# Expert stage of an attention, mixture-of-experts and feed-forward chain: the weight splits move behind the activation's halves, operand tiles are loaded a unit ahead, and the unit count is read sooner

## The chip, the cores and the metric

The kernel runs on one core of a Trainium2 chip. A core has five engines, each working through its own queue of instructions in order: PE (matrix products), DVE (element-wise work on vectors), ACT (activations and copies), POOL and SP. Here SP only issues transfers and reads registers. The metric is the device time of one execution in microseconds (us); the lower the better.

## The reference

Three steps follow each other: attention with pooled keys, a mixture of 8 experts that takes one expert per token, and a gated feed-forward layer.

```python
def _moe_ref(x, modality_id, w_gate, modality_bias, w1, w2):      # x: 4608 tokens x 512
    logits = x @ w_gate + modality_bias[modality_id]
    e_idx = np.argmax(logits, axis=1)
    ...                                                            # gate_w: softmax at e_idx
    for e in range(8):
        mask = e_idx == e
        h = np.maximum(x[mask] @ w1[e], 0.0)                       # w1[e]: 512 x 1024
        out[mask] = gate_w[mask, None] * (h @ w2[e])               # w2[e]: 1024 x 512

def _moe2_ref(x, w_in, w_out):                                     # w_in 512 x 2048, w_out 2048 x 512
    h = x @ w_in
    g = h * np.clip(h + 3.0, 0.0, 6.0) / 6.0
    return g @ w_out
```

The weights w_in and w_out arrive as 64-bit floats, so they have to be converted on the chip.

## The kernel before

The attention stage ends at about 197 us and the feed-forward stage starts at about 651 us. Between them lies the expert stage, in which the change is made. Tokens of one expert stand together in rows of a table, and `unit` works on 400 of them with one expert's weights. This input gives 12 units: one written out ahead of a loop, eight passes of the loop `For_i`, and three written out behind it. How many passes there are stands in `nun`, a number that DVE computes during the first unit; each engine loads it into a register ahead of the loop.

Full precision is kept by splitting each operand into a rounded part and a remainder: `split` has ACT write the rounded part (`wh`, `xhi`, `hi`) and DVE the remainder (`wl`, `xlo`, `lo`), and a product is three MATMULs. A unit has eight steps f = 0 to 7, over slices of 128 hidden columns. In step f:

- `w_dma(f+3)`: SP issues the loads of slice f+3 of the two weight matrices into one of two buffers `ws`; it waits until the split of slice f+1 has read that buffer.
- `w_split(f+2)`: two pairs of `wh` (ACT) and `wl` (DVE), one for w1 and one for w2, into one of four buffers.
- `h_mm(f)`: 12 MATMULs into `ph`, then `hi` on ACT (the activation's rounded half) and `lo` on DVE (its remainder).
- `y_mm(f-1)`: 12 MATMULs that add slice f-1 to the four outputs `y`. It needs hi and lo of f-1.

So PE does h(0), h(1), y(0), h(2), y(1), ..., h(7), y(6), y(7). At f = 7 the next unit's tokens are transposed in four chunks (`transp`), two ahead of y(6) and two behind it. Each writes one of two PSUM tiles `pt`, and `xhi`, `xlo` (and for the first chunk also the copy `tkr`) must have read a tile before the third and fourth chunk may write it. A unit ends with four copies `yo` (two on ACT, two on DVE). PE's last MATMUL of a unit is the last of y(7).

Work for the feed-forward stage is woven in. In the loop each pass converts one slice of w_in: `conv_load` loads it as two tiles `cs`, `conv` makes two lists of 13 small operations, and `unit` runs up to five of them per step. In the two units behind the loop `wo_load` and `wo_conv` do the same for six tiles of w_out (`ds`, nine operations each). The order within each engine is the order in which this code is written.

Of the kernel before, what the change touches and what calls it, by code (L numbers as in the profile page):

```python
# [781 lines left out]
def moe1(tc, g, xr_d, tok_d, y_d, s_d, w1, w2, w_in):  # L782
# [4 lines left out]
    def pool(n, b, st=es_l, **kw):  # L787
        return st.enter_context(tc.tile_pool(name=n, bufs=b, reuse_waits="tile", **kw))
# [21 lines left out]
        s.pst = pool("pst", 2, es_p, space=PSUM)  # L810

    def open3():
        s.cv = pool("cv", 1)
        s.st2 = pool("cst", 2)

    def ps():
        return s.pst.tile([P, 512], F32, name="pt", tag="pt")
# [17 lines left out]
    def transp(c, pt):  # L835
        for t in range(4):
            nc.tensor.transpose(pt[:, t * T4:(t + 1) * T4], s.xg[:, t, c * P:(c + 1) * P], g.idn[:T4, :T4])
        if c == 0:
            nc.tensor.transpose(pt[0:4, NW:NW + T4], s.xg[:, :, GC + 1], g.idn[:T4, :T4])
        split(nc, s.xhi[c], s.xlo[c], pt[:, 0:NW])  # L840
        if c == 0:
            nc.scalar.copy(s.tkr, pt[0:4, NW:NW + T4])
# [7 lines left out]
    def w_split(f, cs=range(2)):  # L850
        for c in cs:
            split(nc, s.wh[f % 4][:, c], s.wl[f % 4][:, c], s.ws[f % 2][:, c])
# [12 lines left out]
        return nc.sync.dma_start(y_d.rearrange("(d p) n -> p d n", p=P)[:, :, bass.ds(col, NW)], s.yo)  # L865

    def conv_load(c, h):
        t = s.st2.tile([P, 4, P, 2], I32, name="cs", tag="cs")
        for b, ks, n in ((t[:, 1:3], slice(h, 4, 2), 0), (t[:, 0:4:3], slice(h, 4, 2), F2)):
            nc.sync.dma_start(b.rearrange("p k f w -> p k (f w)"), w32[:, ks, bass.ds(2 * P * c + n, 2 * P)])  # L870
        return t

    def conv(t):

        sh = [P, 4, P]
        a, m, ex = (s.cv.tile(sh, I32, name=n, tag=n) for n in ("a", "m", "ex"))
        x = s.cv.tile([P, 8, P], F32, name="wx", tag="wx")
        o = s.cv.tile([P, 7, 2, P], F32R, name="wq", tag="wq", bufs=2)
        v = nc.vector
        tt = lambda d, p, q, op: lambda: v.tensor_tensor(x[:, d], x[:, p], x[:, q], op=op)  # L880
        return o, f64_parts(nc, g, t[:, :, :, 1], t[:, :, :, 0], a, m, ex) + [
            lambda: v.tensor_tensor(x[:, 0:4], a.bitcast(F32), m.bitcast(F32), op=ALU.add),
            tt(4, 0, 3, ALU.add),
            tt(6, 1, 0, ALU.subtract),
            tt(5, 4, 1, ALU.subtract),
            tt(7, 2, 5, ALU.subtract),
            lambda: nc.scalar.copy(o[:, :, 0], x[:, 1:8]),
            lambda: v.tensor_tensor(o[:, :, 1], x[:, 1:8], o[:, :, 0].bitcast(F32), op=ALU.subtract),
        ]
# [1 line left out]
    def conv_store(o, c, h):  # L891
        nc.sync.dma_start(s_d[bass.ds(c, 1), :, h].rearrange("o s p x -> p (o s) x"), o.bitcast(F32).rearrange("p s w f -> p s (w f)"))

    def unit(i, first=False, last=False, tail=None, quad=None, fs=()):
        e = s.e0 if first else reg(0, i, E - 1)
        yps = [s.psy.tile([P, NW], F32, name=f"y{d}", tag=f"y{d}") for d in range(4)]
        hh = {}
        cs = {}

        def h_mm(f):  # L900
            j = f % 4
            n = 0
            ph = s.psh.tile([P, NW], F32, name="ph", tag="ph")
            for k in range(4):
                for a, b in ((s.wh, s.xhi), (s.wh, s.xlo), (s.wl, s.xhi)):
                    nc.tensor.matmul(ph, a[j][:, 0, k * P:(k + 1) * P], b[k], start=(n == 0), stop=(n == 11))  # L906
                    n += 1
            hi = s.hp.tile([P, NW], F32R, name="hi", tag="hi")
            lo = s.hp.tile([P, NW], F32R, name="lo", tag="lo")
            nc.scalar.activation(hi, ph, AF.Relu)  # L910
            nc.vector.scalar_tensor_tensor(lo, ph, 0.0, hi.bitcast(F32), op0=ALU.max, op1=ALU.subtract)  # L911
            hh[f] = (hi, lo)

        def y_mm(f):
            j = f % 4
            hi, lo = hh.pop(f)
            for d in range(4):
                for n, (a, b) in enumerate(((s.wh, hi), (s.wl, hi), (s.wh, lo))):
                    nc.tensor.matmul(yps[d], a[j][:, 1, d * P:(d + 1) * P], b, start=(f == 0 and n == 0), stop=(f == 7 and n == 2))  # L919

        lx = LX if first else 1
        parts = {LX: (0, 1, 2, 3)} if first else {1: (0,), 2: (1,), 3: (2,), 4: (3,)}
        ops = []
        for f in range(8):
            if first and f == 0:
                w_dma(e, 2)
            if f == lx and not last:
                en = reg(0, i + 1, E - 1)
            if f < 5 or not last:
                w_dma(e if f < 5 else en, (f + 3) % 8)  # L930
            if f == 0 and not first:
                col = reg(5, i, NT)
                if quad is not None:
                    cc = nc.values_load(g.tab[0:1, 6, bass.ds(quad, 1)], engines=(ET.SP,), min_val=0, max_val=NQ - 1)
            if f < 6 or not last:
                w_split((f + 2) % 8)
            h_mm(f)
            if f in parts and not last:
                load_x(i + 1, parts[f])
            if f - 1 in parts and not last:  # L940
                gate_x(parts[f - 1])
            if f == 2:
                store_tok(NT if first else reg(5, i + 1, NT))
            if f == 3 and not first:
                store_y(col)
            if f == 7 and not last:
                for c in range(2):
                    transp(c, ps())
            if f > 0:
                y_mm(f - 1)  # L950
            if tail and next(tail, None):
                open3()
            if last:
                if f in (1, 2):
                    g.y_load(0, f - 1)
                if f == 3:
                    ops = g.y_ops(0)
                if f == 3:
                    nc.sync.dma_start(g.tk, tok_d[NW:NW + NT].rearrange("(c p) -> c p", p=P))
                if f == 7:  # L960
                    pt = ps()
                    nc.tensor.transpose(pt[:, 0:NT // P], g.tk, g.idn[0:NT // P, 0:NT // P])
                    nc.vector.tensor_copy(g.tki, pt[:, 0:NT // P])
                if f >= 1:
                    g.s_load()
                if f >= 3:
                    for _ in range(3):
                        if ops:
                            ops.pop(0)()
                if f >= 6:  # L970
                    g.wo_load(REST[f - 6])
            elif quad is not None:
                if f == 0:
                    cs[0], cs[1] = conv_load(cc, 0), conv_load(cc, 1)
                if f == 1:
                    co, ops = conv(cs.pop(0))
                if f == 4:
                    c1_, ops = conv(cs.pop(1))
                for _ in range(5):
                    if ops:  # L980
                        ops.pop(0)()
                if f == 4:
                    conv_store(co, cc, 0)
                if f == 7:
                    conv_store(c1_, cc, 1)
            elif fs:
                if f in (0, 1, 4):
                    g.wo_load(fs[min(f, 2)])
                if f in (1, 3, 5):
                    ops += g.wo_conv(fs[f // 2])  # L990
                for _ in range(5):
                    if ops:
                        ops.pop(0)()
        if not last:
            for c in range(2, 4):
                transp(c, ps())
        y_mm(7)
        for d in range(4):
            (nc.scalar.copy if d % 2 else nc.vector.tensor_copy)(s.yo[:, d], yps[d])

    def run(tail):
        open_ps()
        unit(0, first=True, tail=tail)
        n_l = nc.values_load(g.nun, min_val=NQ, max_val=NQ + 8)
        with tc.For_i(0, n_l, 1, iteration_sync="reg_based") as i:
            unit(i + 1, quad=i)
        es_l.close()
        g.open_d()
        unit(n_l + 1, fs=EARLY[0:3])
        unit(n_l + 2, fs=EARLY[3:6])  # L1010
        unit(n_l + 3, last=True)
        store_y(reg(5, n_l + 4, NT))
        es_p.close()
        es_r.close()
# [171 lines left out]
def chunk_kernel(ctx, tc, q, k, v, mid, w_gate, mbias, w1, w2, w_in, w_out, out):  # L1186
# [8 lines left out]
    with tc.manual_schedule(engines={ET.PE, ET.Activation, ET.DVE, ET.SP}):  # L1195
# [5 lines left out]
            g.sp, g.yp, p, g.cv = pool("ds"), pool("dy"), pool("dw"), pool("dcv")  # L1201
            g.wo = {f: p.tile([P, 2, DM], F32R, name=f"wo{f}") for f in EARLY}

        g.open_d = open_d
        g.tk = g.cp.tile([NT // P, P], F32, name="tk")
        g.tki = g.cp.tile([P, NT // P], I32, name="tki")
        g.raw, g.yc = {}, {}
# [41 lines left out]
        g.sts = {}  # L1249

        def wo_load(f):
            t = g.yp.tile([P, DM, 2], I32, name="ds", tag="ds", bufs=2)
            nc.sync.dma_start(t.rearrange("p f w -> p (f w)"), w_out.bitcast(I32)[f * P:(f + 1) * P])
            g.sts[f] = t

# [40 lines left out]
```

## Time and profile before

| what | us |
|---|---|
| median of 3 runs | 1419.81 (1418.35 to 1423.13) |
| profiled execution, its own time | 1420.61 |
| its span, from the first to the last instruction | 1418.9 |
| PE busy | 1371.0 (97%) |
| DVE busy | 940.7 (66%) |
| ACT busy | 624.1 (44%) |
| a loop pass, from a unit's last MATMUL to the next unit's last | 36.42 to 36.44 |

The profile is one execution. Its own time is 1.7 us longer than its span, and 0.8 us above the median of the runs. A busy PE is not a PE at its peak, because the matmuls overlap; so for the expert stage the time of whole units says more than PE's busy share.

### The profile page before, as it was taken

How to read it: one execution, taken by the hardware profiler on the slowest of the kernel's cores; microseconds unless marked ns; L12 is line 12 of the kernel's file. 1: busy time of each engine (PE TensorE's matmuls, PEld its weight loads, DVE VectorE, ACT ScalarE, POOL GpSimd, SP SyncE). 2: the span in 40 equal slices, each digit the busy share in tenths (PEclk: the TensorE clock that was granted, in tenths of full speed). 3: DMA queues.
4: the chain of work that ended last, by engine and by line, in shares of the span. 5: the costliest groups of instructions: out<-in, count | busy, mean ns of one | idle time of the engine just before them, and what ended most of it. 6: DMA issues, size and time to landing. Idle time of an engine off the chain costs nothing.

```text
span 1418.9 us, 24229 instructions
## 1 busy us (share of the span) xinstructions
PE 1371.0 (97%) x7685; PEld 1263.2 (89%) x7685; DVE 940.7 (66%) x1922; ACT 624.1 (44%) x1262; POOL 156.5 (11%) x190
## 2 busy tenths in 40 slices
PE   7898999999999999999999999999999999999997
PEld 5787889899999999898888888888889888888886
DVE  6988884888888886777787445645654564455443
ACT  3666663555555554444444333423432342244222
POOL 3232341111111111100000100100010010001001
PEclk8999999999999999999999999999999999999999
DMA  9996265777778776665654544553454355445431
GB/s 247 305 299 190 91 198 161 237 242 242 240 243 248 241 242 199 198 210 179 202 162 119 183 137 123 157 165 114 122 181 141 113 150 176 119 116 166 115 116 67
DMA packets 229238, 253.87 MB, mean 179 GB/s; under 512 B 19225, under 2 KB 191293, under 8 KB 229149
## 3 DMA queue, kind: packets, MB, share of 16 engines
q1 hardware_dynamic: 223388, 232.64, 54.7%
q0 software_dynamic: 5760, 20.10, 3.9%
q8 instruction: 50, 0.82, 0.3%
q14 instruction: 40, 0.32, 0.1%
HBM read 206.21 MB, written 46.47 MB: 178 GB/s over the span
## 4 chain that ended last, share of the span: by engine, by line
issue 56%; POOL 2%; DVE 2%; DMA 1%; PE 1%; ACT 0%; SPq 0%; POOLq 0%; DVEq 0%; ACTq 0%
POOL out_dram L1049 2%; DMA ds<-in_moe_w_out_dram 1%; DVE wl L755 1%; DMA ws<-in_moe_w_dram 0%; PE ph L906 0%; DVE lo L911 0%; PE y L919 0%; DVE da L766 0%; DVE dex L777 0%; DVE dm L764 0%; DVE dm L765 0%; DVE dm L768 0%; SPq L820 0%; ACT dex L763 0%; POOLq L1291 0%
## 5 line engine op out<-in xcount | busy, mean ns | idle before, releaser
L1070 PE MATMUL hps<-yc,sq 128*128 128x384 f32 x2004 | 405.1, 337 | 3.3 <-ACT s L1111 1.6
L1070 PEld LDWEIGHTS hps<-yc,sq 128*128 128x128 f32 x2004 | 358.3, 188 | 37.3 <-ACT s L1111 5.5
L1060 PE MATMUL ops<-wo,gh 128*128 128x512 f32 x1152 | 358.5, 392 | 0.0
L1060 PEld LDWEIGHTS ops<-wo,gh 128*128 128x128 f32 x1152 | 211.4, 188 | 23.1
L1060 PE MATMUL ops<-wo,gl 128*128 128x512 f32 x576 | 228.7, 397 | 0.0
L1082 ACT ACTIVATE r<-c,three 128x384 f32<-128x384 f32 x144 | 88.8, 617 | 208.4 <-DVE c L1092 208.0
L755 DVE TENSOR_TENSOR wl<-ws,wh 128x512 fp32r<-128x512 f32 x192 | 132.8, 728 | 35.5 <-ACT wh L754 32.1
L1086 ACT CAST gh<-r 128x384 fp32r<-128x384 f32 x192 | 98.7, 514 | 129.4 <-DVE r L1083 128.0
L754 ACT CAST wh<-ws 128x512 fp32r<-128x512 f32 x192 | 114.5, 619 | 72.2 <-DMA ws<-in_moe_w_dram 54.4
L919 PE MATMUL y<-lo,wh 128*128 128x400 f32 x384 | 133.6, 348 | 1.8 <-DVE lo L911 1.7
L919 PE MATMUL y<-hi,wh 128*128 128x400 f32 x384 | 134.6, 350 | 0.6 <-ACT hi L910 0.5
L906 PE MATMUL ph<-xhi,wh 128*128 128x400 f32 x384 | 132.3, 344 | 2.0 <-PEq L1291 1.2
L906 PE MATMUL ph<-xlo,wh 128*128 128x400 f32 x384 | 132.8, 346 | 0.0
L906 PE MATMUL ph<-xhi,wl 128*128 128x400 f32 x384 | 132.6, 345 | 0.0
L919 PE MATMUL y<-hi,wl 128*128 128x400 f32 x384 | 132.0, 344 | 0.0
L1060 PEld LDWEIGHTS ops<-wo,gl 128*128 128x128 f32 x576 | 107.9, 187 | 23.1
L1087 DVE TENSOR_TENSOR gl<-r,gh 128x384 fp32r<-128x384 f32 x192 | 106.5, 554 | 27.6 <-ACT gh L1086 23.2
L1049 POOL DMA_INDIRECT out_dram<-osb,tki x36 | 35.3, 982 | 777.3 <-ACT osb L1047 745.4
L1083 DVE SCALAR_TENSOR_TENSOR r<-r,c 128x384 f32<-128x384 f32 x144 | 80.4, 558 | 55.1 <-ACT r L1082 53.2
L829 POOL TENSOR_TENSOR cxg<-cxg 100x512 f32<-100x512 f32 x48 | 56.7, 1184 | 348.4 <-PE ph L906 182.6
L1083 DVE SCALAR_TENSOR_TENSOR r<-r,hps 128x384 f32<-128x384 f32 x48 | 26.6, 554 | 97.7 <-ACT r L1082 97.6
L1082 ACT ACTIVATE r<-hps,three 128x384 f32<-128x384 f32 x48 | 27.9, 581 | 131.6 <-PE hps L1070 131.5
(214 smaller groups left out, 1903.6 us busy)
## 6 DMA issues: line engine op xcount, KB each, us to landing
sq<-sd SPq DMA_DIRECT2D x336, 256.0 KB
ws<-in_moe_w_dram SPq DMA_DIRECT2D x192, 256.0 KB, 3.9
sd<-wq SPq DMA_DIRECT2D x16, 896.0 KB
cxg<-xr SPq DMA_DIRECT2D x44, 225.8 KB
yd<-yo SPq DMA_DIRECT2D x12, 800.0 KB
yr<-yd SPq DMA_DIRECT2D x12, 768.0 KB
kv<-in_k_dram SPq DMA_DIRECT2D x16, 512.0 KB
kv<-in_v_dram SPq DMA_DIRECT2D x16, 512.0 KB
```

What stands on the lines that cost most here:

```text
L754: nc.scalar.copy(hi, src)
L755: nc.vector.tensor_tensor(lo, src, hi.bitcast(F32), op=ALU.subtract)
L829: nc.gpsimd.tensor_tensor(s.xg[:, t, 0:DM].rearrange("p (h x) -> p h x", x=D), v, s.xg[:, t, GC:GC + 1].unsqueeze(2).to_broadcast([T4, H, ...
L906: nc.tensor.matmul(ph, a[j][:, 0, k * P:(k + 1) * P], b[k], start=(n == 0), stop=(n == 11))
L919: nc.tensor.matmul(yps[d], a[j][:, 1, d * P:(d + 1) * P], b, start=(f == 0 and n == 0), stop=(f == 7 and n == 2))
L1049: i_ = nc.gpsimd.indirect_dma_start(out=out, out_offset=bass.IndirectOffsetOnAxis(ap=tki[:, c:c + 1], axis=0), in_=o, in_offset=None).ins
L1060: nc.tensor.matmul(pso[t_], gt[a][:, t * P:(t + 1) * P], wo[f][:, b], start=(q == 0 and fh == th and n == 0), stop=(q == NQ - 1 and fh != ...
L1070: nc.tensor.matmul(ps, w[:, kk, a * P:(a + 1) * P], y[:, b, kk], start=(start and n == 0), stop=(n == 5), skip_group_check=True)
L1082: a_.activation(r, c, AF.Relu, bias=g.three)
L1083: v.scalar_tensor_tensor(r, r, 6.0, c, op0=ALU.min, op1=ALU.mult)
L1086: a_.copy(gh, r)
L1087: late.append(lambda: v.tensor_tensor(gl, r, gh.bitcast(F32), op=ALU.subtract))
```

## The change

Three things change in `unit`. The weight split of a step is written behind `h_mm`, so `hi` and `lo` stand ahead of it on ACT and DVE; at f = 7 it stands behind the first two transposed chunks. The tiles `cs` for a pass are loaded during the unit before it: the first two, together with two tiles of w_out, in the first unit at f = 3, and each following one as soon as its buffer has been read; the conversions then start at f = 0, and run four operations per step in the w_out units instead of five. And `nun` is loaded into the registers at f = 6 of the first unit. The two `ds` buffers get a pool of their own, opened early.

```diff
     def open3():
+        g.open_w()
         s.cv = pool("cv", 1)
-        s.st2 = pool("cst", 2)
+        p = pool("cst", 1)
+        s.cs = [p.tile([P, 4, P, 2], I32, name=f"cs{h}") for h in range(2)]
...
     def conv_load(c, h):
-        t = s.st2.tile([P, 4, P, 2], I32, name="cs", tag="cs")
+        t = s.cs[h]
...
-                    cc = nc.values_load(g.tab[0:1, 6, bass.ds(quad, 1)], engines=(ET.SP,), min_val=0, max_val=NQ - 1)
-            if f < 6 or not last:
-                w_split((f + 2) % 8)
+                    cc, cn = (nc.values_load(g.tab[0:1, 6, bass.ds(quad + d, 1)], engines=(ET.SP,), min_val=0, max_val=NQ - 1) for d in range(2))
             h_mm(f)
+            if f < 7:
+                if f < 6 or not last:
+                    w_split((f + 2) % 8)
...
             if f == 7 and not last:
                 for c in range(2):
                     transp(c, ps())
+                w_split(1)
             if f > 0:
                 y_mm(f - 1)
             if tail and next(tail, None):
                 open3()
+                for h in range(2):
+                    conv_load(0, h)
+                for w in EARLY[0:2]:
+                    g.wo_load(w)
+            if first and f == 6:
+                s.n_l = nc.values_load(g.nun, min_val=NQ, max_val=NQ + 8)
...
             elif quad is not None:
-                if f == 0:
-                    cs[0], cs[1] = conv_load(cc, 0), conv_load(cc, 1)
-                if f == 1:
-                    co, ops = conv(cs.pop(0))
-                if f == 4:
-                    c1_, ops = conv(cs.pop(1))
+                if f in (0, 3):
+                    co, ops = conv(s.cs[f // 3])
                 for _ in range(5):
                     if ops:
                         ops.pop(0)()
-                if f == 4:
-                    conv_store(co, cc, 0)
-                if f == 7:
-                    conv_store(c1_, cc, 1)
-            elif fs:
-                if f in (0, 1, 4):
-                    g.wo_load(fs[min(f, 2)])
-                if f in (1, 3, 5):
-                    ops += g.wo_conv(fs[f // 2])
-                for _ in range(5):
+                if f in (3, 6):
+                    conv_store(cq, cc, f // 3 - 1)
+                    conv_load(cn, f // 3 - 1)
+                if f in (2, 5):
+                    cq = co
+            elif fs is not None:
+                if f in (0, 2, 4):
+                    ops += g.wo_conv(EARLY[3 * fs + f // 2])
+                for _ in range(4):
                     if ops:
                         ops.pop(0)()
+                n = 3 * fs + f // 2 + 1
+                if f in (2, 4, 6) and n < len(EARLY):
+                    g.wo_load(EARLY[n])
...
     def run(tail):
         open_ps()
         unit(0, first=True, tail=tail)
-        n_l = nc.values_load(g.nun, min_val=NQ, max_val=NQ + 8)
+        n_l = s.n_l
```

On DVE, at the end of the first unit behind the loop (the ninth after the first), the program of before has these rows; `ds`, `da`, `dm`, `dex` and `wo` belong to the conversion of w_out:

```order
L911 SCALAR_TENSOR_TENSOR lo<-ph,hi 128x400
L768 SCALAR_TENSOR_TENSOR dm<-ds,dex 128x512
L777 TENSOR_TENSOR dex<-da,wo_3809 128x512
L778 TENSOR_TENSOR wo_3809<-dex,dm 128x512
L755 TENSOR_TENSOR wl_2597<-ws_2092,wh_2593 128x512 x2
L911 SCALAR_TENSOR_TENSOR lo<-ph,hi 128x400
L755 TENSOR_TENSOR xlo_2087<-pt,xhi_2083 128x400
L755 TENSOR_TENSOR xlo_2088<-pt,xhi_2084 128x400
```

The changed program has these at the same place:

```order
L910 SCALAR_TENSOR_TENSOR lo<-ph,hi 128x400
L755 TENSOR_TENSOR wl_2596<-ws_2091,wh_2592 128x512 x2
L777 TENSOR_TENSOR dex<-da,wo_3830 128x512
L778 TENSOR_TENSOR wo_3830<-dex,dm 128x512
L910 SCALAR_TENSOR_TENSOR lo<-ph,hi 128x400
L755 TENSOR_TENSOR xlo_2087<-pt,xhi_2083 128x400
L755 TENSOR_TENSOR xlo_2088<-pt,xhi_2084 128x400
L755 TENSOR_TENSOR wl_2597<-ws_2092,wh_2593 128x512 x2
```

Between the last two `lo` there were three conversion operations and two `wl`; now two `wl` and two operations, and the step's own `wl` pair stands behind the first two `xlo`.

On ACT, at the head of a loop pass, the program of before has these rows (`ex` is the first operation of a w_in conversion):

```order
L754 CAST wh_2594<-ws_2091 128x512
L754 ISA
L754 CAST wh_2594<-ws_2091 128x512
L910 ISA
L910 ACTIVATE hi<-ph 128x400
L754 CAST wh_2595<-ws_2092 128x512
L754 REGISTER_ALU
L754 CAST wh_2595<-ws_2092 128x512
L910 ISA
L910 ACTIVATE hi<-ph 128x400
L763 REGISTER_ALU
L763 ACTIVATE ex<-cs 128x512
```

and the changed program these:

```order
L909 ACTIVATE hi<-ph 128x400
L754 CAST wh_2594<-ws_2091 128x512 x2
L763 ACTIVATE ex<-cs_3077 128x512
L909 ISA
L909 ACTIVATE hi<-ph 128x400
L754 CAST wh_2595<-ws_2092 128x512 x2
L909 ISA
L909 ACTIVATE hi<-ph 128x400
```

Each `hi` now comes ahead of the `wh` pair of its step, and `ex` one step sooner.

On SP, in the first unit, these rows of before lie between the loads of slices 6 and 7:

```order
L848 DMA ws_2091<-in_moe_w_dram 128x512
L820 TENSOR_LOAD tab
L820 ISA x2
L846 ISA
L846 DMA ws_2092<-in_moe_w_dram 128x4x128
```

and these in the changed program:

```order
L850 DMA ws_2091<-in_moe_w_dram 128x512
L872 DMA cs_3077<-in_moe_w_in_dram 128x2x256 x2
L872 DMA cs_3078<-in_moe_w_in_dram 128x2x256 x2
L1261 DMA ds<-in_moe_w_out_dram 128x1024 x2
L822 TENSOR_LOAD tab
L822 ISA x2
L848 ISA
L848 DMA ws_2092<-in_moe_w_dram 128x4x128
```

Six transfers, 2 MB in all, are issued there that were issued later before.

## Rows read from the trace of the kernel before

**Rows 1.** The page, part 1: busy us (share) x instructions of each engine.

```profile
PE 1371.0 (97%) x7685; PEld 1263.2 (89%) x7685; DVE 940.7 (66%) x1922; ACT 624.1 (44%) x1262; POOL 156.5 (11%) x190
```

**Rows 2.** Units 0, 1, 2, 9, 10: length; busy PE, PEld, DVE, ACT, POOL; clock; DMA.

```profile
197.34:237.85 40.51, 38.74 (x228) 36.13 (x224) 27.40 (x97) 18.41 (x42) 10.55 (x10) 1.00 0.56 171
237.85:279.44 41.59, 37.93 (x211) 36.01 (x211) 30.17 (x53) 18.87 (x35) 4.93 (x4) 1.00 0.74 225
279.44:315.86 36.42, 36.42 (x211) 36.32 (x210) 29.69 (x53) 19.12 (x35) 4.43 (x4) 1.00 0.78 243
...
534.46:577.87 43.41, 39.03 (x210) 37.01 (x210) 31.13 (x52) 19.52 (x37) 4.91 (x4) 0.97 0.66 199
577.87:616.04 38.17, 37.41 (x210) 36.82 (x210) 31.67 (x52) 19.36 (x37) 5.25 (x4) 0.98 0.60 184
```

**Rows 3.** Timeline, PE, unit 0: start us, us, instruction [idle before <-releaser].

```profile
203.46 0.45 PE L919 MATMUL y<-lo,wh 128*128 128x400 f32 x1 [0.59 <-DVE lo L911]
...
231.99 0.45 PE L919 MATMUL y<-lo,wh 128*128 128x400 f32 x1 [0.18 <-DVE lo L911]
```

**Rows 4.** Timeline, all engines, from unit 0 into the loop.

```profile
238.23 0.49 ACT L999 COPY yo<-y 128x400 f32<-128x400 f32 x1 [0.60 <-PE y L919]
...
238.85 0.45 PE L906 MATMUL ph<-xhi,wh 128*128 128x400 f32 x1 [0.65 <-ACTq L1005]
```

**Rows 5.** Timeline, ACT, unit 1 (the loop's first pass).

```profile
248.13 0.66 ACT L763 ACTIVATE ex<-cs 128x512 f32<-128x512 f32 x1 [3.96 <-DMA cs<-in_moe_w_in_dram]
```

**Rows 6.** Timeline, PE, unit 1: the product behind it, and the transposes.

```profile
252.71 0.45 PE L919 MATMUL y<-hi,wh 128*128 128x400 f32 x1 [0.51 <-ACT hi L910]
...
275.97 0.56 PE L837 MATMUL pt<-idn,cxg 100*128 100x100 f32 x4 [1.24 <-ACT tkr L842]
```

**Rows 7.** Timeline, all engines, end of unit 9.

```profile
567.39 0.35 PE L906 MATMUL ph<-xhi,wl 128*128 128x400 f32 x1
...
572.06 0.57 DVE L911 SCALAR_TENSOR_TENSOR lo<-ph,hi 128x400 fp32r<-128x400 f32 x1
...
573.43 0.57 PE L837 MATMUL pt<-idn,cxg 100*128 100x100 f32 x4 [2.46 <-ACT tkr L842]
```

**Rows 8.** Windows, the stretch after that wait.

```profile
575.00:580.00 5.00, 5.00 (x20) 5.00 (x20) 2.27 (x5) 2.52 (x5) 0.00 (x0) 0.66 0.27 91
```

**Rows 9.** Timeline, PE, out of the loop into unit 9.

```profile
536.02 0.42 PE L906 MATMUL ph<-xhi,wh 128*128 128x400 f32 x1 [1.21 <-PEq L1291]
```

**Rows 10.** Timeline, PE, the transposes at the end of unit 10.

```profile
613.61 0.56 PE L837 MATMUL pt<-idn,cxg 100*128 100x100 f32 x4 [0.43 <-DVE xlo L755]
```

**Rows 11.** Timeline, DVE, steps 0 and 1 of a loop pass (unit 6).

```profile
428.48 0.57 DVE L911 SCALAR_TENSOR_TENSOR lo<-ph,hi 128x400 fp32r<-128x400 f32 x1 [0.28 <-ACT hi L910]
428.97 1.28 DVE L755 TENSOR_TENSOR wl<-ws,wh 128x512 fp32r<-128x512 f32 x2
```

**Rows 12.** Timeline, PE, same pass: first MATMUL of h(2).

```profile
431.92 0.34 PE L906 MATMUL ph<-xhi,wh 128*128 128x400 f32 x1
```

**Rows 13.** Timeline, SP, unit 0: loads of slice 7 and of the next tokens.

```profile
217.45 0.38 SPq L846 DMA_DIRECT2D ws<-in_moe_w_dram  x1
...
219.27 5.60 SPq L824 DMA_DIRECT2D cxg<-xr  x4
```

**Rows 14.** Timeline, DVE, unit 0: the last operation on the unit table.

```profile
214.32 0.15 DVE L744 TENSOR_TENSOR urr<-urr,udf 32x4 f32<-32x4 f32 x1
```

**Rows 15.** Windows, unit 0: the transfers.

```profile
216.00:218.00 2.00, 2.00 (x13) 2.00 (x12) 1.91 (x6) 0.51 (x1) 0.00 (x0) 1.00 0.00 0
218.00:226.00 8.00, 8.00 (x46) 8.00 (x45) 2.23 (x4) 1.64 (x3) 2.13 (x2) 1.00 0.55 154
```

**Rows 16.** Tile cs, 230 to 300 us: time of its 256 KB loads.

```profile
DMA to landing us min/median/max: 2.9/4.7/5.9
```

**Rows 17.** Timeline, ACT and PE, unit 0: split and product of slice 7.

```profile
221.74 0.62 ACT L754 CAST wh<-ws 128x512 fp32r<-128x512 f32 x1 [3.99 <-DMA ws<-in_moe_w_dram]
...
227.93 0.35 PE L906 MATMUL ph<-xhi,wh 128*128 128x400 f32 x1
```

More of the change, by code (lines that the diff above doesn't have):

```diff
@@ L867, in conv_load @@
     def conv_load(c, h):
-        t = s.st2.tile([P, 4, P, 2], I32, name="cs", tag="cs")
+        t = s.cs[h]
         for b, ks, n in ((t[:, 1:3], slice(h, 4, 2), 0), (t[:, 0:4:3], slice(h, 4, 2), F2)):
             nc.sync.dma_start(b.rearrange("p k f w -> p k (f w)"), w32[:, ks, bass.ds(2 * P * c + n, 2 * P)])
-        return t
     def conv(t):
@@ L892, in conv_store, with unit @@
         nc.sync.dma_start(s_d[bass.ds(c, 1), :, h].rearrange("o s p x -> p (o s) x"), o.bitcast(F32).rearrange("p s w f -> p s (w f)"))
-    def unit(i, first=False, last=False, tail=None, quad=None, fs=()):
+    def unit(i, first=False, last=False, tail=None, quad=None, fs=None):
         e = s.e0 if first else reg(0, i, E - 1)
@@ L897, in unit @@
         hh = {}
-        cs = {}
         def h_mm(f):
@@ L1008, in run @@
         g.open_d()
-        unit(n_l + 1, fs=EARLY[0:3])
-        unit(n_l + 2, fs=EARLY[3:6])
+        unit(n_l + 1, fs=0)
+        unit(n_l + 2, fs=1)
         unit(n_l + 3, last=True)
@@ L1202, in open_d, with open_w @@
             g.wo = {f: p.tile([P, 2, DM], F32R, name=f"wo{f}") for f in EARLY}
-        g.open_d = open_d
+        def open_w():
+            g.dst = ctx.enter_context(tc.tile_pool(name="dst", bufs=2, reuse_waits="tile"))
+        g.open_d, g.open_w = open_d, open_w
         g.tk = g.cp.tile([NT // P, P], F32, name="tk")
@@ L1251, in wo_load @@
         def wo_load(f):
-            t = g.yp.tile([P, DM, 2], I32, name="ds", tag="ds", bufs=2)
+            t = g.dst.tile([P, DM, 2], I32, name="ds", tag="ds")
             nc.sync.dma_start(t.rearrange("p f w -> p (f w)"), w_out.bitcast(I32)[f * P:(f + 1) * P])
```

## The prediction

> **What bounds the kernel now.** I read the page first: PE is busy for 97% of the span, every other engine for less [rows 1]. So nothing can be won that doesn't shorten PE's waits, and the question is where those are. I therefore cut the expert stage into windows at each unit's last MATMUL [rows 2]. Unit 2, a loop pass, takes 36.42 us with PE busy for all of it, and the other passes behind the first take 36.42 to 36.44. That is what a unit costs when nothing makes PE wait. Against 36.43, unit 1 has 5.16 us too much, unit 9 has 6.98 and unit 10 has 1.74; unit 0, which carries other work as well, shows 1.77 us of idle PE. Units 2 to 8 have nothing to give back.
>
> Next I read PE's own timeline for the releaser of each wait. 211 MATMULs start in 36.42 us, so 0.17 us apart, while one lasts 0.34; a wait printed as x therefore costs about x + 0.16.
>
> - Unit 0: twice a second product waits for lo, 0.59 and 0.18 us [rows 3].
> - Into the loop: 0.65 us until ACT has signalled; its last copy yo starts at 238.23 and PE goes on at 238.85 [rows 4]. Between the two, ACT's queue holds the load of nun.
> - Unit 1: ACT waits 3.96 us for the first cs tile [rows 5]; behind that stand the next wh pair and the hi for which PE then waits. At the end the third transposed chunk waits 1.24 us for tkr [rows 6].
> - Unit 9: the product of step 7 has its last MATMUL at 567.39, but DVE comes to its lo only at 572.06, since conversions and two wl pairs stand ahead of it. xlo, tkr and PE's third chunk follow from there, and PE waits 2.46 us [rows 7]. After that wait PE's granted clock is 0.66 over 5 us, a mix of its two levels, full and half [rows 8]: 0.34 x 5 = 1.7 us of MATMUL time lost, part of it in unit 10's head.
> - Out of the loop into unit 9: 1.21 us for PE's sequencer [rows 9], which the change leaves.
> - Unit 10: the same transposes wait 0.43 us [rows 10], and as much again for the chunk before.
>
> **The change part by part.** *Splits behind hi and lo.* No instruction is added. A lo no longer stands behind a wl pair (1.28 us, [rows 11]), a hi no longer behind a wh pair that waits for a load. In unit 0 I count both late lo: 0.59 + 0.18 + 2 x 0.16 = 1.1, and 0.1 for the hi beside the second: 1.2 us. Bounds: 0, if DVE's backlog there comes from other work, and 2.7, all 1.77 us of idle PE with 0.16 for each of some six waits. The transposes of unit 0 I leave as they are.
>
> The price is that each split starts later, behind lo, and what is late next is the product that needs it. In a pass lo(0) starts at 428.48 and the next DVE operation at 428.97; a wl pair of 1.28 from there ends at 430.25 [rows 11], and h(2), which needs it, starts at 431.92 [rows 12]: 1.7 us to spare. Step 0 is the tightest, for from step 1 on a further product of 12 MATMULs (12 x 0.18 = 2.2 us) lies between. The load behind a split also starts later; two steps (four products, 8.7 us) lie between a buffer's splits, and the loads of such a size took at most 5.9 us [rows 16]. So I cost this at nothing for units 2 to 8.
>
> *Tiles a unit ahead.* In unit 1 the wait of 3.96 us on ACT goes, and with it the late hi and lo; the pass should then run as the others do. Of 5.16 us the loop's entry is 0.82 (0.65 + 0.16), so 4.35 us here. The lower bound is 2.9, if the wait at the transposes (1.24 + 0.16) comes back. In unit 9 the conversions start a step or two earlier and none is left at f = 7 but what the rows of the order show; the lo of step 7 stands right behind two of them. Of 6.98 us, 1.37 stay at the loop's exit (1.21 + 0.16), and I leave 0.3 for small waits: 5.3 us. Unit 10: all 1.7. Lower bounds: 1.3 and 0.5, if the long wait (2.46 + 0.16) and the clock's 1.7 stay in unit 9 and the transposes still wait in unit 10.
>
> The transfers themselves are the same ones earlier, plus one pass's 1 MB that nobody reads; the loop's transfers use 0.78 of the engines' time [rows 2]. Each pass reads one more register on SP. Four reads with their issues took 5.60 us [rows 13], so at most 1.4 us each. It is hidden while the load of slice 3 isn't needed before step 3; uncovered it would be 8 x 1.4 = 11 us.
>
> *nun sooner.* ACT's signal can follow its last copy's start instead of a load behind it. I take 0.5 of the 0.82 us (bounds 0 and 0.82). The load itself now stands ahead of hi(7) in unit 0, where ACT is busy for 18.41 of 40.51 us [rows 2].
>
> **Sum:** 1.2 + 4.35 + 0.5 + 5.3 + 1.7 = 13.05 us; with all upper bounds 15.2. The profiled execution took 1420.6, so 1407.5. It stands 0.8 above the median of the runs; I keep that as an allowance for waits a new order leaves.
>
> **The rivals.**
>
> *The 2 MB in unit 0 delay slice 7 (1410 to 1411.5).* Six loads now stand on SP ahead of it. The second cs tile lies where the unit table's scratch lay, so its loads wait for the table's last operation at 214.32 [rows 14]. Four issues remain then, of 0.38 us and a little between them, and the register read; slice 7 goes out at about 218.5 instead of 217.45 [rows 13]. The transfers were idle from 216 to 218 and half idle until 226 [rows 15]. At 243 / 0.78 = 311 GB/s 2 MB take 6.7 us, at 243 they take 8.6 [rows 2]. From 215.5 that ends at 222.2 or 224.1; slice 7's first half follows 1 us later, and its split takes 1.3: 224.5 to 226.5. Its product starts at 227.93 [rows 17], or 0.75 sooner with the first gain. So I expect no wait. A load was slower by 3 us when others stood around it (2.9 against 5.9, [rows 16]); so much again gives a wait of 2.3, and if the clock falls as in unit 9, 4.0. The Trainium skill's page "DMA: Bandwidth & Descriptors", section "Queues, rings and completion order", says that one DMA engine takes the descriptors of a ring in order. By that rule slice 7 can't overtake the 2 MB, which speaks for this rival; the spread of the cs loads agrees, and by it alone the time lies between my sum and 1411.5.
>
> *The transposes still wait (1414).* The wh pair now stands between the xhi of the second and third chunk. If the chain lo, xlo, tkr stays as late in units 1, 9 and 10 because DVE's work is no smaller (31 us of 43 and 38, [rows 2]), 1.4 + 4.3 + 1.1 = 6.8 us of the gain are lost. Against it: after lo(7) only xlo is left, and the conversions are over.
>
> *A loop pass pays (slower, 1421 or more).* If the later splits make h(2), or another product, wait in each of eight passes, 1.63 us per pass eat the sum. It decides from the point where a wl pair ends 3.3 us later than worked out above (1.7 to spare, and 1.63). SP's extra read could do it. Against it: DVE is busy for 29.7 of 36.4 us in a pass, so 6.7 us are spare; waiting for lo(0) at its head costs about 2.
>
> *The stalls only move (no change, 1417 to 1420).* DVE's total is the same, and each unit's end could collect what its middle gave.
>
> **How the numbers follow.** Forecast 0.60, slice 7 0.15, transposes 0.10, no change 0.08, slower pass 0.07. A measurement tells from no change what exceeds about 0.3%, 4.3 us. The first three are faster by more: 0.85. The range reaches from all upper bounds (1405) past the slice 7 rival to the transposes' (1414.5); outside are the last two and a little of each tail.
>
> **What would show it.** In the new profile: units 1, 9 and 10 within 0.5 us of 36.9, 38.1 and 36.5 (splits and tiles right); no half clock in unit 9; the entry to the loop at 0.5 us start to start; unit 0 at 39.3. Wrong: any of units 2 to 8 above 36.6, or PE waiting in unit 0 for wl of slice 7.

## The result and the profile after

The changed kernel takes 1426.65 us (median of 7 runs, 1423.92 to 1427.93); the kernel before, timed beside it, 1419.81. The ratio is 1.0058 (95% interval 1.0046 to 1.0071), so it is slower, by 0.6% (6.8 us between the medians), where 12 us less were forecast. The profiled execution has a span of 1424.9 us against 1418.9.

The page of the changed kernel, part 1, answers to [rows 1]:

```profile
PE 1373.1 (96%) x7685; PEld 1261.8 (89%) x7685; DVE 939.2 (66%) x1922; ACT 614.0 (43%) x1262; POOL 153.6 (11%) x190
```

The busy sums tell nothing of 6 us. The windows do, cut at the same place of each unit as in [rows 2]: units 0 and 1, then the passes 2 to 8, and, from the same view asked for other stretches, units 9 and 10.

```profile
196.90:237.47 40.57, 38.46 (x228) 36.49 (x224) 27.82 (x96) 17.81 (x42) 10.99 (x10) 1.00 0.72 223
237.47:275.29 37.82, 37.13 (x210) 36.22 (x210) 29.19 (x53) 18.00 (x35) 4.20 (x4) 1.00 0.76 225
...
546.38:585.83 39.45, 36.91 (x211) 36.31 (x211) 31.73 (x52) 19.11 (x37) 4.95 (x4) 1.00 0.68 205
585.83:622.38 36.55, 36.55 (x210) 36.38 (x210) 31.12 (x52) 18.66 (x37) 4.82 (x4) 1.00 0.59 178
```

```profile
275.29:314.05 38.76, 37.37 (x211) 36.29 (x211) 29.88 (x53) 17.98 (x35) 4.79 (x4) 1.00 0.75 227
314.05:351.64 37.59, 36.87 (x211) 36.26 (x210) 29.49 (x53) 17.99 (x35) 4.35 (x4) 1.00 0.79 234
...
467.25:507.05 39.80, 37.90 (x210) 36.13 (x210) 29.57 (x53) 17.99 (x35) 4.38 (x4) 1.00 0.73 223
...
sum 271.09, PE 261.30 PEld 253.57 DVE 207.88 ACT 125.94 POOL 30.58; mean PE 37.33 PEld 36.22 DVE 29.70 ACT 17.99 POOL 4.37
```

Units 1, 9 and 10 are shorter by 3.8, 4.0 and 1.6 us, as meant. But the seven passes that had nothing to give back take 271.1 us together instead of 255.0: 2.3 us each, 16.1 in all. No engine works more in them, the clock is 1.00 and the share of the transfers is 0.73 to 0.79, against 0.78 in unit 2 of before. So it is waiting, and the next step is to see what for. ACT in unit 7, from hi of step 5 on:

```profile
489.44 0.51 ACT L909 ACTIVATE hi<-ph 128x400 fp32r<-128x400 f32 x1 [2.75 <-PE ph L905]
495.49 1.29 ACT L754 CAST wh<-ws 128x512 fp32r<-128x512 f32 x2 [5.54 <-DMA ws<-in_moe_w_dram]
498.59 0.94 ACT L887 CAST wq<-wx 128x896 fp32r<-128x896 f32 x1 [1.81 <-DVE wx L880]
499.44 0.50 ACT L909 ACTIVATE hi<-ph 128x400 fp32r<-128x400 f32 x1
```

ACT waits 5.54 us for the load of slice 7. The same wait, 3.7 to 4.8 us, stands at step 5 of each other pass. Behind it in ACT's order are a conversion's wq, which needs DVE's wx, and then hi(6); on DVE the wl pair, wx, wq and lo(6) queue up in the same way. PE pays at the end of the unit, at five places in a row: h(7) waits for the wh of slice 7, y(6) for hi(6) and for lo(6), and the two late transposes for tkr and xlo.

```profile
496.16 0.45 PE L905 MATMUL ph<-xhi,wh 128*128 128x400 f32 x1 [0.22 <-ACT wh L754]
499.99 0.45 PE L918 MATMUL y<-hi,wh 128*128 128x400 f32 x1 [0.24 <-ACT hi L909]
501.20 0.45 PE L918 MATMUL y<-lo,wh 128*128 128x400 f32 x1 [0.58 <-DVE lo L910]
503.62 0.56 PE L839 MATMUL pt<-idn,cxg 100*128 100x100 f32 x4 [0.33 <-ACT tkr L844]
504.62 0.56 PE L839 MATMUL pt<-idn,cxg 100*128 100x100 f32 x4 [0.43 <-DVE xlo L755]
```

PE's own waits are small and name ACT and DVE; a reader of this view alone would blame the order on those engines. SP's timeline shows what the load of slice 7 (the two `ws` rows at the end) stands behind:

```profile
482.85 0.41 SPq L867 DMA_DIRECT2D yd<-yo  x1
483.52 0.40 SPq L892 DMA_DIRECT2D sd<-wq  x1
484.13 2.62 SPq L872 DMA_DIRECT2D cs<-in_moe_w_in_dram  x2
487.03 1.14 SPq L848 DMA_DIRECT2D ws<-in_moe_w_dram  x1
488.44 1.07 SPq L850 DMA_DIRECT2D ws<-in_moe_w_dram  x1
```

The store of y (0.8 MB), the store of the converted w_in (0.9) and the reload of cs (0.5) go out in a row, 2.2 MB, and then slice 7. Its buffer had been free since the wl pair of slice 5 ended, at about 484.8, 2.2 us before SP came to it. In the same pass of before only the store of y stands there, and the other store goes out behind slice 7:

```profile
474.02 0.41 SPq L865 DMA_DIRECT2D yd<-yo  x1
475.37 0.38 SPq L846 DMA_DIRECT2D ws<-in_moe_w_dram  x1
476.01 1.05 SPq L848 DMA_DIRECT2D ws<-in_moe_w_dram  x1
478.44 0.34 SPq L824 DMA_DIRECT2D cxg<-xr  x1
479.12 0.41 SPq L892 DMA_DIRECT2D sd<-wq  x1
```

While the changed kernel's 2.2 MB move, the windows show the transfers busy at a share of about 1.0 for 12 us (the last two columns are their share and GB/s); a mean of 0.73 over the pass hides that:

```profile
480.00:484.00 4.00, 4.00 (x24) 4.00 (x23) 2.99 (x5) 2.94 (x5) 1.04 (x1) 1.00 0.57 179
484.00:488.00 4.00, 4.00 (x24) 4.00 (x23) 3.80 (x8) 1.53 (x3) 1.04 (x1) 1.00 1.03 364
488.00:492.00 4.00, 4.00 (x24) 4.00 (x23) 3.68 (x9) 0.51 (x1) 0.00 (x0) 1.00 1.00 284
492.00:496.00 4.00, 3.94 (x22) 3.61 (x20) 0.00 (x0) 0.51 (x1) 0.00 (x0) 1.00 0.96 248
```

That made three theories. **Q (queue):** the transfers that the change puts in a row ahead of slice 7 make its load late. **S (splits):** the splits behind hi and lo leave ACT and DVE late at a unit's end, whatever the transfers do. **D:** the conversions, begun a step sooner, do.

### The profile page after: what moved, and what is told of

Its sections match the earlier page's. It is cut to its first block, busy times and chain, and to the rows that moved or that the text cites. A ratio compares the mean times of both kernels' runs of the same rounds, so it can differ in the third digit from the quotient of the medians.

```text
span 1424.9 us, 24218 instructions
## 1 busy us (share of the span) xinstructions
PE 1373.1 (96%) x7685; PEld 1261.8 (89%) x7685; DVE 939.2 (66%) x1922; ACT 614.0 (43%) x1262; POOL 153.6 (11%) x190
## 4 chain that ended last, share of the span: by engine, by line
issue 55%; PE 2%; POOL 2%; DVE 1%; DMA 1%; ACT 0%; POOLq 0%; SPq 0%; DVEq 0%; ACTq 0%
POOL out_dram L1054 2%; PE ph L905 1%; PE y L918 1%; DMA ws<-in_moe_w_dram 1%; DVE wl L755 0%; DVE dex L777 0%; DVE lo L910 0%; DVE dm L764 0%; DVE wo L778 0%; POOLq L1299 0%; ACT wh L754 0%; DVE xlo L755 0%; DVE dm L765 0%; DVE dm L768 0%; ACT dex L763 0%
## 5 line engine op out<-in xcount | busy, mean ns | idle before, releaser
L755 DVE TENSOR_TENSOR wl<-ws,wh 128x512 fp32r<-128x512 f32 x192 | 127.4, 698 | 32.0 <-ACT wh L754 31.5
L754 ACT CAST wh<-ws 128x512 fp32r<-128x512 f32 x192 | 110.7, 618 | 48.3 <-DMA ws<-in_moe_w_dram 47.7
L909 ACT ACTIVATE hi<-ph 128x400 fp32r<-128x400 f32 x96 | 48.4, 504 | 111.3 <-PE ph L905 110.5
L831 POOL TENSOR_TENSOR cxg<-cxg 100x512 f32<-100x512 f32 x48 | 53.4, 1116 | 362.6 <-PE y L918 192.9
```

Of the source, the lines that this page charges most:

```text
L754: nc.scalar.copy(hi, src)
L755: nc.vector.tensor_tensor(lo, src, hi.bitcast(F32), op=ALU.subtract)
L831: nc.gpsimd.tensor_tensor(s.xg[:, t, 0:DM].rearrange("p (h x) -> p h x", x=D), v, s.xg[:, t, GC:GC + 1].unsqueeze(2).to_broadcast([T4, H, ...
```

## The experiments

Ratios are to the kernel before, timed beside each; on the chips of the three groups of experiments it took 1425.22, 1417.72 and 1417.81 us, so ratios are compared, not times.

**1. The reloads one step later.**

```diff
                 if f in (3, 6):
                     conv_store(cq, cc, f // 3 - 1)
+                if f in (4, 7):
                     conv_load(cn, f // 3 - 1)
```

> The changed kernel, but a pass reloads the cs tiles at f = 4 and f = 7, one step behind the stores instead of right behind them at f = 3 and f = 6. Theory Q (queue): in every pass ACT waits 3.7 to 5.5 us at step 5 for the load of slice 7, because y's store (0.8 MB), the wq store (0.9 MB) and the cs reload (0.5 MB) are issued in a row ahead of it; the engine that moves data is busy to 1.0 for 12 us there. With 0.5 MB less ahead of it (some 1.7 us at 300 GB/s) the wait falls to 2 to 3 us, units 2 to 8 to 36.6 to 37.5, and the time to 1411 to 1420. Theory S (the splits stand behind hi and lo, which leaves DVE and ACT late at the unit's end whatever the transfers do) and theory D (the conversions begin a step earlier): the passes stay at 37.6 to 39.8 and the time at 1424 to 1429.

Ratio 0.9945 (0.9925 to 0.9965). Units 2 to 8 take 36.42 to 36.60. In unit 7 slice 7 now goes out ahead of the reload, and ACT waits 2.69 us for it, which no product feels:

```profile
478.95 0.41 SPq L867 DMA_DIRECT2D yd<-yo  x1
479.62 0.40 SPq L892 DMA_DIRECT2D sd<-wq  x1
480.67 0.94 SPq L848 DMA_DIRECT2D ws<-in_moe_w_dram  x1
...
485.76 0.98 SPq L872 DMA_DIRECT2D cs<-in_moe_w_in_dram  x2
```

```profile
488.57 0.62 ACT L754 CAST wh<-ws 128x512 fp32r<-128x512 f32 x1 [2.69 <-DMA ws<-in_moe_w_dram]
```

S and D fall as causes of their own: split order and conversions are as in the changed kernel, and the loss is gone. So is SP's second register read per pass as a cause, which this kernel keeps.

**2. The splits back.**

```diff
-            h_mm(f)
-            if f < 7:
-                if f < 6 or not last:
-                    w_split((f + 2) % 8)
+            if f < 6 or not last:
+                w_split((f + 2) % 8)
+            h_mm(f)
...
                     transp(c, ps())
-                w_split(1)
```

> The changed kernel with its weight splits back ahead of the step's product, everything else as changed. Theory Q: the load of slice 7 still lands late, now with hi and lo of step 5 behind its split, so units 2 to 8 stay at 37.5 or more: 1422 to 1434. Theory S: units 2 to 8 return to 36.4 and the time falls to 1408 to 1413. Theory D: as the changed kernel, 1424 to 1429.

Ratio 1.0071 (1.0049 to 1.0092), passes of 37.6 to 39.1. The late load alone is enough; its wait now holds hi(5) too (unit 7):

```profile
502.02 1.30 ACT L754 CAST wh<-ws 128x512 fp32r<-128x512 f32 x2 [7.46 <-DMA ws<-in_moe_w_dram]
503.23 0.50 ACT L909 ACTIVATE hi<-ph 128x400 fp32r<-128x400 f32 x1
```

**3. Only the splits**, in the kernel before (the diff above the other way round).

> The kernel before with nothing but the weight splits moved behind hi and lo (at f = 7 behind two transposed chunks). Theory Q: stores and loads stand in the queue as before, so units 2 to 8 stay at 36.4 to 36.6; unit 9 loses its long wait in part; 1414 to 1420. Theory S: units 2 to 8 take 38 to 39 as in the changed kernel, 1430 or more. Theory D: as theory Q.

Ratio 0.9981 (0.9968 to 0.9994). Units 2 to 8 take 36.42 to 36.82, unit 0 39.81 (0.7 less than before). Unit 1 takes 39.03, 2.6 less than before, with the cs tiles loaded where they were. Unit 10 takes 39.23, 1.1 more. And unit 9 stays at 43.07; its transposes still wait 2.8 us start to start: with the conversions where they were, the split order alone doesn't get DVE there sooner. That part of the expectation missed.

```profile
573.71 0.73 PE L837 MATMUL pt<-idn,cxg 100*128 100x100 f32 x4 [2.46 <-ACT tkr L842]
```

**4. The store of y sooner**, at f = 1 instead of f = 3.

> The changed kernel, but the store of the last unit's y (0.8 MB) is issued at f = 1 instead of f = 3. Theory Q: 0.8 MB fewer stand ahead of the load of slice 7 (2.6 us at 300 GB/s); ACT's wait at step 5 falls to 1 to 2.5 us, units 2 to 8 to 36.5 to 37.2, the time to 1408 to 1416. Theories S and D: no change, 1424 to 1429.

Ratio 0.9967 (0.9953 to 0.9982); units 2 to 8 at 36.42 to 36.54. Taking another of the three transfers out of the row cures the passes as well, with a wait of 2.86 us left on ACT in unit 7. Units 9 and 10 got longer here (41.08 and 40.40) in the profiled execution, which is the slowest of its seven (1425.15); why stays open.

**5. The first unit's 2 MB spread**, with the later reloads. Why: in experiment 1 unit 0 took 42.0 us. In the changed kernel's unit 0 PE's timeline names a gate on POOL, not slice 7, as the wait:

```profile
231.08 0.30 PE L839 MATMUL pt<-idn,cxg 100*128 100x100 f32 x1 [0.70 <-POOL cxg L831]
```

and POOL's timeline the tokens, which stand on SP behind slice 7 and so behind the 2 MB as well; the first gate starts at 226.24 (223.50 in the kernel before):

```profile
226.24 4.79 POOL L831 TENSOR_TENSOR cxg<-cxg 100x512 f32<-100x512 f32 x4 [13.94 <-DMA cxg<-xr]
```

```diff
                 open3()
-                for h in range(2):
-                    conv_load(0, h)
-                for w in EARLY[0:2]:
-                    g.wo_load(w)
+            if first and f > 3:
+                if f < 6:
+                    conv_load(0, f - 4)
+                else:
+                    g.wo_load(EARLY[f - 6])
...
+                if f in (4, 7):
                     conv_load(cn, f // 3 - 1)
```

> The changed kernel with the reloads at f = 4 and f = 7 (as in the first experiment), and the 2 MB of the first unit spread: the two cs tiles at the end of f = 4 and f = 5, the two w_out tiles at f = 6 and f = 7, all behind the load of the next unit's tokens. Theory Q (what stands in the queue ahead of a load decides): the tokens' gate ends in time for the transposes, unit 0 falls from 42.0 (first experiment) to 39.5 to 40.2, units 2 to 8 stay at 36.4 to 36.6, and the ratio to the kernel before goes from 0.9945 to 0.991 to 0.9935. Rival: unit 0 is long for another reason (the table's work), it stays at 41.5 or more and the ratio at 0.9945; or the loads, now later, make the first pass wait for cs, and unit 1 goes above 38.

Ratio 0.9952 (0.9939 to 0.9966), unit 0 40.96: a miss. The kernel of experiment 1, timed again in experiment 10, has 0.9945 and 41.01, so the spread gained nothing. The tokens came in time, but slice 0 of the next unit now stood behind cs, and ACT waited 4.78 us for it, with hi(7) and xhi behind. The wait had moved by one load.

```profile
231.78 1.30 ACT L754 CAST wh<-ws 128x512 fp32r<-128x512 f32 x2 [4.78 <-DMA ws<-in_moe_w_dram]
```

**6. The same with the splits back.**

> The kernel of the spread loads with its weight splits back ahead of the step's product. It says what the split order is worth once no load is late. My own working gave the splits 1.2 us in unit 0 and most of the 1.7 us in unit 10, so 2 to 4 us slower than the spread kernel (ratio 0.993 to 0.996). Rival: with the loads in time the order is worth nothing, the two differ by less than 1 us. Second rival: the later splits cost in the passes after all, and this one is faster by 1 us or more.

Ratio 0.9993 (0.9984 to 1.0002) against 0.9952: 0.0041 of 1417.72, 5.8 us, where 2 to 4 were expected. The split order is worth more here than I gave it, but not, as I meant to ask, with every load in time: slice 0 is late in both kernels. Of the 5.8 us 3.5 stand in unit 0. There the old order makes hi wait behind the late load's split, and PE 2.64 us for that hi; the windows give a clock of 0.59, a mix of its full and half level, for the 4 us behind it:

```profile
233.55 0.45 PE L918 MATMUL y<-hi,wh 128*128 128x400 f32 x1 [2.64 <-ACT hi L909]
```

```profile
234.00:238.00 4.00, 3.59 (x11) 2.86 (x10) 2.65 (x5) 2.14 (x5) 0.00 (x0) 0.59 1.07 375
```

**7. The reload on another queue.** The changed kernel, its passes' reloads issued by ACT at the same places (`nc.scalar.dma_start`).

> The changed kernel with the passes' cs reloads issued by ACT on a queue of its own, at the same places of the program (f = 3 and f = 6); the stores stay on SP. It tells order in the queue from bytes in all. If the load of slice 7 is late because it stands behind the reload in one queue, the reload no longer delays it, ACT's wait at step 5 falls below 3 us, and units 2 to 8 to 36.4 to 37.0 (ratio 0.995 to 0.999). If the bytes that move at that time decide, wherever they are queued, the wait stays near 4 us and units 2 to 8 at 37.6 or more (ratio 1.004 or more).

Ratio 1.0023 (1.0011 to 1.0035), passes of 36.97 to 38.18: between the two forecasts, so neither held. SP reaches slice 7 sooner (482.17, 17.5 us into unit 7 instead of 19.8), but the load takes longer, and ACT's wait stays:

```profile
492.10 1.34 ACT L754 CAST wh<-ws 128x512 fp32r<-128x512 f32 x2 [4.72 <-DMA ws<-in_moe_w_dram]
```

So a queue of its own takes the reload out of SP's issue order, not out of slice 7's way. The Trainium skill, page "DMA: Bandwidth & Descriptors", section "Queues, rings and completion order", says that the queues run on the same 16 engines and that each engine takes turns between the queues that have work; the trace agrees: issued at the same place of unit 7 (17.5 us), the load takes 9.9 us from issue to split here and 7.9 in experiment 1, where the reload goes out 5.1 us behind it.

**8. Small stores.** The changed kernel with one part of seven in each store; the other six are left out.

> The changed kernel, but each store of a converted w_in tile writes one of its seven parts (0.13 MB instead of 0.9), and the feed-forward stage reads that part in place of all seven, as often as before; the rest of the converted weights is left out. SP's order, its waits and the number of instructions stay. If the bytes ahead of slice 7 cost the time: ACT's wait at step 5 falls below 2 us, units 2 to 8 to 36.4 to 36.6, ratio 0.994 to 0.998. If SP itself is the cause (it waits for wq before it issues the store, and the load of slice 7 waits behind it): units 2 to 8 stay at 37.5 or more.

Ratio 0.9945 (0.9929 to 0.9960); five of the seven passes at 36.42 to 36.44, two at 37.05 and 37.16, outside the expected 36.6; why those two stays open. SP issues slice 7 as late as in the changed kernel, 19.7 us into unit 7, and yet it comes in time:

```profile
474.04 2.39 SPq L872 DMA_DIRECT2D cs<-in_moe_w_in_dram  x2
476.71 0.37 SPq L848 DMA_DIRECT2D ws<-in_moe_w_dram  x1
```

```profile
481.68 0.62 ACT L754 CAST wh<-ws 128x512 fp32r<-128x512 f32 x1 [1.93 <-DMA ws<-in_moe_w_dram]
```

**9 and 10. Spread further, with the later reloads, and experiment 1 again beside it.**

```diff
                 open3()
-                for h in range(2):
-                    conv_load(0, h)
-                for w in EARLY[0:2]:
-                    g.wo_load(w)
+                conv_load(0, 0)
+            if first and f == 6:
+                conv_load(0, 1)
+            if first and f == 7:
+                g.wo_load(EARLY[0])
...
+                if f in (4, 7):
                     conv_load(cn, f // 3 - 1)
...
+                if fs == 0 and f == 0:
+                    g.wo_load(EARLY[1])
```

> The changed kernel with the reloads at f = 4 and f = 7, and in the first unit only the first cs tile issued at f = 3 (the transfers stood idle there before); the second cs tile goes behind the load of the next unit's slice 1 (f = 6), the first w_out tile to f = 7, the second into the first unit behind the loop (f = 0). In the spread kernel slice 0 of the next unit stood behind 1.4 MB and ACT waited 4.8 us for it with hi(7) and xhi behind. Theory Q: neither the tokens nor slice 0 stand behind more than they did before, so the waits at unit 0's transposes fall under 1 us in all, unit 0 to 39.5 to 40.2, the rest as in the first experiment: ratio 0.990 to 0.994. Rival: unit 0 doesn't shorten by moving these loads (its waits come from its own work), 41 or more, ratio 0.9945 to 0.996.

> The kernel of the first experiment (the reloads one step later, the first unit's 2 MB as changed) timed once more beside the one above. By theory Q slower than it by 1 to 3 us, all of it in unit 0, and about 0.9945 of the kernel before again; by the rival equal to it within 1 us.

Ratios 0.9935 (0.9911 to 0.9958) and 0.9945 (0.9929 to 0.9961), 1408.41 and 1409.53 us. By whole times the two can't be told apart; by unit 0 they can, 38.99 (39.5 to 40.2 were expected) against 41.01. Units 0, 1, 2, 9 and 10 of the ninth:

```profile
196.56:235.55 38.99, 38.01 (x227) 36.51 (x224) 27.29 (x96) 17.91 (x42) 10.71 (x10) 1.00 0.72 218
235.55:272.35 36.80, 36.69 (x211) 36.26 (x210) 29.04 (x53) 18.42 (x35) 4.99 (x4) 1.00 0.78 237
272.35:308.79 36.44, 36.44 (x210) 36.34 (x210) 29.86 (x54) 18.42 (x35) 4.17 (x4) 1.00 0.79 246
527.72:566.55 38.83, 37.11 (x210) 36.22 (x210) 31.50 (x52) 19.42 (x37) 4.32 (x4) 1.00 0.70 213
566.55:602.99 36.44, 36.44 (x210) 36.34 (x210) 30.67 (x52) 18.47 (x37) 4.53 (x4) 1.00 0.58 180
```

It is faster than both kernels: 0.65% below the one before.

**All of them in one table.** Slice 7 in unit 7: us from the last MATMUL of unit 6 to the first issue of its load, to its first wh, and between the two; then the length of unit 7 and the mean of units 2 to 8. Its product is due 28.5 us into the unit.

| kernel | issued | split | between | unit 7 | mean |
|---|---|---|---|---|---|
| before | 13.8 | 18.9 | 5.1 | 36.44 | 36.43 |
| 3, only splits | 16.3 | 22.7 | 6.3 | 36.82 | 36.51 |
| changed | 19.8 | 28.2 | 8.5 | 39.81 | 38.73 |
| 1, reload later | 17.5 | 25.4 | 7.9 | 36.60 | 36.47 |
| 4, y sooner | 19.3 | 25.6 | 6.2 | 36.54 | 36.45 |
| 7, other queue | 17.5 | 27.4 | 9.9 | 38.18 | 37.44 |
| 8, small stores | 19.7 | 24.6 | 5.0 | 36.42 | 36.62 |
| 9, spread more | 17.5 | 24.1 | 6.6 | 36.42 | 36.48 |
| 2, splits back | 18.1 | 25.9 | 7.8 | 38.83 | 38.56 |

With the new split order a split up to 25.6 costs next to nothing, at 27.4 1.7 us and at 28.2 3.4 us. Slice 7's own product then starts only 0.4 us late (28.9 us into the unit); the rest is paid at the products and transposes behind it. The last row has the old order, where hi(5) stands behind this split and 25.9 already costs 2.4 us. The split order makes the load 2.5 us later (16.3 against 13.8), the tiles' new places another 3.5 us (19.8 against 16.3; of these, 1.2 remain in experiment 1, where the reload isn't in the row), and behind the 2.2 MB the load takes 8.5 us. (In the kernel before and in experiment 3 the load was there ahead of its split's turn, so their 5.1 and 6.3 are upper bounds of its time.)

## Why the prediction was wrong

**The step that failed** is "So I cost this at nothing for units 2 to 8", together with "The transfers themselves are the same ones earlier". The first set 8.7 us between a buffer's splits against loads of at most 5.9 us. For the split order alone the conclusion holds (experiment 3). But the 8.7 run from split to split, and the load can go out only when wl has read the buffer as well: in experiment 3 6.3 us lie between its issue and the split's turn. And the 5.9 came from cs loads in the order of before; behind the moved transfers slice 7 took 8.5. I weighed the moved transfers by their share over a pass, 0.78 [rows 2], and never wrote down what stands on SP between two loads of `ws` inside a pass. I did so for unit 0 only. Inside a pass the 2.2 MB at about 300 GB/s, the mean of the last three windows of the result, are 7.3 us, and slice 7's own 0.5 MB another 1.7: 9.0, past even the 8.7. The rival "a loop pass pays" came true at 2.3 us per pass, with 1421 or more as its time; but its first place was h(2) and its suspect SP's extra read, and both were wrong.

Term by term, in us, against the units of [rows 2]. The last column is experiment 9, where the loads are in time, so it says whether the other terms were sized rightly:

| term | predicted | changed kernel | experiment 9 |
|---|---|---|---|
| unit 0 | -1.2 | +0.1 | -1.5 |
| unit 1 with the loop's entry | -4.85 | -3.8 | -4.8 |
| units 2 to 8 | 0 | +16.1 | +0.3 |
| unit 9 | -5.3 | -4.0 | -4.6 |
| unit 10 | -1.7 | -1.6 | -1.7 |
| sum | -13.05 | +6.8 | -12.3 |

- **Unit 0.** Slice 7 did what the rival on the 2 MB worked out: split at 225.33 (224.5 to 226.5 expected) and no wait for it. But behind it on SP stood the tokens, and their gate paid for it. The rival followed the queue one load too few. The gain itself is there in experiment 9, where the 2 MB are spread.
- **Unit 1 and nun.** Start to start the loop's entry takes 0.45 us instead of 1.00, as forecast, and ACT's wait for cs [rows 5] is gone. What is missing is the late slice 7, which unit 1 has too (ACT waits 3.67 us for it); experiment 9 gets the forecast -4.8. But I put the 4.35 to the tiles, and experiment 3 gets 2.6 of it by the split order alone.
- **Unit 9.** The long wait of [rows 7] and the lower clock of [rows 8] are gone. Most of what is missing is at the loop's exit, where PE's sequencer took 2.27 us (1.21 in [rows 9]):

```profile
548.99 0.42 PE L905 MATMUL ph<-xhi,wh 128*128 128x400 f32 x1 [2.27 <-PEq L1299]
```

  Start to start that is 2.61 us; it was 2.04 and 2.24 in experiments 5 and 7 and 1.55 to 1.64 in the others, with the same code of PE there. Why stays open. The rest are small waits, for which I left too little: experiment 9, with 1.56 us at the exit, has 1.0 us of them where I left 0.3.
- **Unit 10** and the clock were right.
- **The splits** were right in direction. The two waits for lo [rows 3] are gone, and experiment 3's unit 0 is 0.7 us shorter where I counted 1.2. The larger part I didn't count: where a load is late, the new order keeps hi and lo out from behind it (5.8 us between experiments 5 and 6).

The mechanism behind the changed kernel's time is shown by three edits that each take another transfer out of the row or shrink it, and the loss goes (experiments 1, 4 and 8), by one that keeps the bytes and keeps part of it (7), by one that keeps the row under the old split order and keeps the loss (2), and by one that has the new split order without the row and has no loss (3). How SP's lateness and the bytes divide the loss exactly is not: experiment 7 takes out the first and lengthens the second.

## What to carry to other kernels

When a transfer is moved earlier, list for each just-in-time load what now stands ahead of it on its queue, in bytes, and set that against its deadline; a mean share of the transfers says nothing of it, and another issuing queue doesn't take the bytes away. A prefetch with a whole unit to spare should go behind the urgent load of its step, not ahead of it. Where PE's small waits name ACT or DVE, follow those engines back to their last long wait before blaming their order.

## What the runs showed of the hardware

How long an issue holds SP isn't constant. The pair of cs issues took 2.62 us right behind two stores and 0.98 in experiment 1, 6 us after them; a `ws` issue, 0.38 us in most places, took 2.42 behind the same stores in experiment 7. A burst so pushes back whatever SP has next, beside delaying it on the way. With the reload on a second queue the urgent load went out 2.3 us sooner into the unit, but was split only 0.8 sooner (27.4 against 28.2): from issue to split it took 9.9 us instead of 8.5.
